# Memory layers on full-array attention products, a head-split output projection and one activation table

## Chip, cores and metric

The kernel runs on one core of a Trainium2 chip. The metric is the device time of one execution in microseconds, as the median of several runs. The core has five engines with their own instruction streams: TensorE (PE; its weight loads are listed as PEld), VectorE (DVE), ScalarE (ACT), GpSimd (POOL) and SyncE (SP). In this kernel TensorE writes to eight PSUM banks of 128x512 float32, and ACT and DVE move the results to SBUF.

## The reference

Four layers with residuals, A, B, A, B, on x of 2048x512 in bfloat16, each after a layer norm without weights. B is linear attention with 32 heads of 16. A is attention with a recurrent memory of 8 rows, 32 heads of 128:

```python
mem = mem0                                  # 8 x 512
for s in range(64):                         # segments of 32 tokens
    h = concat([mem, x[32*s:32*s+32]])      # 40 rows
    q, k, v = h @ Wq, h @ Wk, h @ Wv        # 32 heads of 128
    scores = q @ k.T / sqrt(128)
    scores = where((i < 8) | (i >= j), scores, -1e9)   # i: query row, j: key row
    o = softmax(scores) @ v                 # per head
    o = o @ Wo                              # back to 512
    mem = o[:8]; outs.append(o[8:])
```

The memory rows see all 40 rows; token rows see the memory and the tokens up to themselves. Segment s+1 cannot be projected before segment s's memory rows have come out of Wo.

## The kernel before

**Order of the work.** The kernel lists nodes (`_Prog.add`: engine or engines, function, cost, keys read and written, PSUM tiles). `schedule` is run once for each layer and makes a fixed order for each engine: a list scheduler that takes the ready node with the longest tail by the costs given (`c_act`, `c_dve`, `c_pe`, `c_pe4`), places evictions marked ANY on ACT or DVE, and gives out the eight banks. A node that isn't `urgent` needs three free banks to open a new tile. `emit` then writes the engines' programs, with semaphore waits.

**Tiling of a memory layer** (`a_layer`). A step works on a block of 32 rows: the 8 memory rows and the first 24 tokens of its segment. The last 8 tokens of four segments ("left") make a block of their own, done once for a group of four (`left_block`). With M=32 rows a full array is a quarter used, so nearly everything is put into four column strips of 32 (`tile_position=(0, 32*j)`), which in a group of four run side by side. Heads go as head = 8*j + hh, strip j = 0..3, hh = 0..7, in two halves b.

- `project` (L593): four chunks of the 512 inputs by four strips, 512 wide, so 16 matmuls for each of q, k, v and b.
- `transposed` (L610): the evicted projection is transposed, 16 matmuls of 128 wide, and evicted into qT or kT.
- `mem_attention`: `scores` (L623) of the memory queries against block and left keys, 32 matmuls of 8 wide a half; exponential (L672) on 128x64; sums by matmuls with masks of ones (`sums`, L677 and L680); reciprocal (L684), product (L686); then L689 spreads the probabilities over the four strips with zeros elsewhere (a 4 times wider product with a mask), so that `pvm` (L700, L703) can contract all 128 rows: 32 matmuls a half.
- `x_attention`: the same for the 24+8 token queries: scores 64 matmuls of 24 and 8 wide, exponential (L722), mask (L724), sums (L731, L734), Ln (L738) and Exp of its negative (L740) as reciprocal, products (L742, L744), spreading (L748, twice), and `pvx` 64 matmuls (L759, L763). Its result is for the next step's `out_block`.
- `out_proj` (L781): 32 heads by four strips of 128 output columns: 128 matmuls of 128 wide into a bank of 128x128, evicted to outW in bf16. `next_mem` (L798) selects the 8 memory rows, transposed, into the next block hT. `residual` (L816, L819) does the left output projection and the sum with x once for a group.

Evictions are made by the helper `copy`, so they show as L472 (ACT) or L473 (DVE). Each change between Ln and Exp or Copy brings an ACT_TABLE_LOAD, listed with the line of the activation that needs it.

**Linear layers** (`b_layer`): per tile of 128 tokens a layer norm (transposes L575, in strips), projections with the full array (L885, L892), exponentials and key-value products (L908); then KV and sum products (L927, L933), transposes (L950) and the output projection (L959).

Of the kernel before, what the change touches and what calls it, by code (L numbers as in the profile page):

```python
# [6 lines left out]
F32 = mybir.dt.float32  # L7
ACTF = mybir.ActivationFunctionType
ALU = mybir.AluOpType
# [6 lines left out]
HOP = 0.06  # L16

# [34 lines left out]
class _Node:  # L52
    __slots__ = ("engs", "fn", "cost", "sync", "order", "tiles", "dsem", "dval", "eng", "start", "done",
                 "tail", "sig", "val", "waits", "know", "idx", "nsucc", "succ", "nleft", "urgent")


class _Prog:
    def __init__(self, nc, banks):
        self.nc = nc
        self.nodes = []  # L60
        self.res = {}
        self.banks = banks
        self.dma_tot = {}
        self.sems = {}
        self.done_nodes = []
        self.committed = []
        self.now = {e: 0.0 for e in ENGINES}
        self.bank_owner = [None] * len(banks)
        self.last = {e: None for e in ENGINES}

# [3 lines left out]
    def add(self, engs, fn, cost, reads=(), writes=(), tiles=(), dsem=None, urgent=False):  # L74
        nd = _Node()
        nd.engs = (engs,) if isinstance(engs, str) else tuple(engs)
        nd.cost = cost if isinstance(cost, dict) else {e: cost for e in nd.engs}
        nd.fn = fn
        nd.sync = set()
# [38 lines left out]
    def schedule(self):  # L118
# [72 lines left out]
        def pick_for(e):  # L191
# [7 lines left out]
            while ready[e]:  # L199
# [14 lines left out]
                pick = nd  # L214
                break
# [4 lines left out]
        while n_left:  # L220
# [42 lines left out]
            nd.start = max(tn, rtime(nd))  # L263
            nd.done = nd.start + nd.cost[e]
# [95 lines left out]
def _build_kernel(nc, A_x, A_mem0, A_Wq, A_Wk, A_Wv, A_Wo, A_seg_len, B_wqkv, B_wo, out):  # L360
# [31 lines left out]
    id_sb = sb("id_sb", [128, 128])  # L392
    bo_sb = sb("bo_sb", [128, 128])
    bol_sb = sb("bol_sb", [128, 4, 128])
    bm_sb = sb("bm_sb", [128, 4])
    bm8_sb = sb("bm8_sb", [128, 4, 8, 4])
    mx_sb = sb("mx_sb", [128, 32])
    ml_sb = sb("ml_sb", [128, 32])
    idz_sb = sb("idz_sb", [128, 16, 32])
    selm_sb = sb("selm_sb", [128, 4, 8])  # L400
    maskbd_sb = sb("maskbd_sb", [128, 128])
    onehot8_sb = sb("onehot8_sb", [128, 8], F32)
    A8_sb = sb("A8_sb", [128, 128])
    epsb_sb = sb("epsb_sb", [128, 1], F32)
    mem0_sb = sb("mem0_sb", [128, D])
    memT0_sb = sb("memT0_sb", [128, 4, M])
    st_sb = sb("st_sb", [128, 2, 16], F32)
    xln_sb = sb("xln_sb", [128, 2, D])


    ARENA_N = 29248
# [14 lines left out]
    NI = 5  # L426
    hT = av(3 * 5 * 4 * 32).rearrange("p (r b c x) -> p r b c x", r=3, b=5, c=4)
# [3 lines left out]
    qT = av(2 * 1024).rearrange("p (r h j x) -> p r h j x", r=2, h=8, j=4)  # L431
# [4 lines left out]
    oTl = av(2 * 1024).rearrange("p (r n x) -> p r n x", r=2, n=32)  # L436
    Pm = av(2 * 64).rearrange("p (r a q) -> p r a q", r=2, a=2)
    PRm = av(2 * 64).rearrange("p (r a q) -> p r a q", r=2, a=2)
    Pbm = av(2 * 256).rearrange("p (r a q) -> p r a q", r=2, a=2)
    Px = av(2 * 256).rearrange("p (r h q) -> p r h q", r=2, h=8)  # L440
    PLL = av(2 * 256).rearrange("p (r h q) -> p r h q", r=2, h=8)
    PRx = av(8 * 40).rearrange("p (h q) -> p h q", h=8)
    Pbx = av(8 * 4 * 40).rearrange("p (h j q) -> p h j q", h=8, j=4)
    outW = av(8 * 128).rearrange("p (r x) -> p r x", r=8)
    outWl = av(2 * 128).rearrange("p (r x) -> p r x", r=2)
    Rm = av(2 * 32, F32).rearrange("p (r q) -> p r q", r=2)
    Rx = av(256, F32).rearrange("p (h q) -> p h q", h=8)
    Lx = av(256, F32).rearrange("p (h q) -> p h q", h=8)
# [14 lines left out]
    rd_sb = av(2 * 32, F32).rearrange("p (r x) -> p r x", r=2)  # L463

# [19 lines left out]
    add("sp", lambda s: s.dma_start(mem0_sb[0:M, :], A_mem0[0]), 2.0, writes=["mem0"], dsem="dmem")  # L484
# [5 lines left out]


# [3 lines left out]
    def sel(ap, op, fill, base, pattern, cm, key):  # L495
        pool(lambda g: g.affine_select(out=ap, in_=ap, compare_op=op, fill=fill, base=base, pattern=pattern,
                                       channel_multiplier=cm), writes=[key], reads=[key])
# [4 lines left out]
    pool(lambda g: g.memset(epsb_sb[:, :], EPS_LN), ["epsb"])  # L502

# [3 lines left out]
    pool(lambda g: g.memset(bm_sb[:, :], 1.0), ["bm"])  # L507
    sel(bm_sb[:, :], GE, 0.0, 0, [[-32, 4]], 1, "bm")
    sel(bm_sb[:, :], GE, 0.0, 31, [[32, 4]], -1, "bm")
    pool(lambda g: g.memset(bol_sb[:, :, :], 1.0), ["bol"])  # L510
    sel(bol_sb[:, :, :], GE, 0.0, 0, [[-8, 4], [-32, 4], [0, 32]], 1, "bol")
    sel(bol_sb[:, :, :], GE, 0.0, 7, [[8, 4], [32, 4], [0, 32]], -1, "bol")
    pool(lambda g: g.memset(bm8_sb[:, :, :, :], 1.0), ["bm8"])
    sel(bm8_sb[:, :, 0:4, :], GE, 0.0, 0, [[0, 4], [0, 4], [-32, 4]], 1, "bm8")
    sel(bm8_sb[:, :, 0:4, :], GE, 0.0, 31, [[0, 4], [0, 4], [32, 4]], -1, "bm8")
    sel(bm8_sb[:, :, 4:8, :], GE, 0.0, 0, [[-8, 4], [0, 4], [-32, 4]], 1, "bm8")
    sel(bm8_sb[:, :, 4:8, :], GE, 0.0, 7, [[8, 4], [0, 4], [32, 4]], -1, "bm8")
# [10 lines left out]
    pool(lambda g: g.memset(idz_sb[:, :, :], 0.0), ["idz"])  # L528
    sel(idz_sb[:, :, 24:32], ALU.not_equal, 1.0, 0, [[-8, 16], [-1, 8]], 1, "idz")
    pool(lambda g: g.memset(selm_sb[:, :, :], 0.0), ["selm"])  # L530
    sel(selm_sb[:, :, :], ALU.not_equal, 1.0, 0, [[-32, 4], [-1, 8]], 1, "selm")
    pool(lambda g: g.memset(A8_sb[:, :], 1.0), ["A8"])
    sel(A8_sb[0:8, :], GE, 0.0, 0, [[1, 128]], -16, "A8")
    sel(A8_sb[0:8, :], GE, 0.0, 15, [[-1, 128]], 16, "A8")
# [3 lines left out]
        reads=["A8"], tiles=[tl])  # L538
# [3 lines left out]
        reads=["A8", "id"], tiles=[tl])  # L542
# [7 lines left out]
    add("pe", _m0, 0.2, reads=["mem0", "id"], tiles=[tl])  # L550
# [6 lines left out]
    def layernorm(t):  # L557
        k = ln_no[0] % 2
# [13 lines left out]
        def tr(pe):  # L572
            for c in range(4):
                for q in range(4):
                    r = pe.transpose(tl.bf16()[32 * q:32 * q + 32, 128 * c:128 * c + 128],  # L575
                                     xln_sb[:, k, 128 * c + 32 * q:128 * c + 32 * q + 32], id_sb[:, :],
                                     tile_position=(0, 32 * q))
            return r
        add("pe", tr, c_pe4(16, 128), reads=[("xln", k), "id"], tiles=[tl])
# [3 lines left out]
    def a_layer(layer):  # L583
# [3 lines left out]
        def project(W, key, blk, bkeys, b, urgent):  # L587
            tl = P.tile()
            for c in range(4):
# [6 lines left out]
                add("pe", mm, c_pe4(4, 512), reads=[key] + bkeys, tiles=[tl], urgent=urgent)  # L596
            return tl

        def transposed(W, key, blk, bkeys, b, dst, dkey, urgent):
# [4 lines left out]
            evac(img[:, k, :], lambda: tl.f32()[:, :], 512, tiles=[tl], writes=[("img", k)], urgent=urgent)  # L604
            tt = P.tile()

            def tr(pe):
                for i in range(4):
                    for q in range(4):
                        r = pe.transpose(tt.bf16()[32 * q:32 * q + 32, 128 * i:128 * i + 128],  # L610
                                         img[:, k, 128 * i + 32 * q:128 * i + 32 * q + 32], id_sb[:, :],
                                         tile_position=(0, 32 * q))
                return r
            add("pe", tr, c_pe4(16, 128), reads=[("img", k), "id"], tiles=[tt], urgent=urgent)
            evac(dst.rearrange("p h j x -> p (h j x)"), lambda: tt.bf16()[:, 0:512], 512, tiles=[tt], writes=[dkey],
                 rate=2, urgent=urgent)

        def scores(tl, col, lhs, lhs_keys, rhs, rhs_keys, hhs, w, urgent):

            def mm(pe):  # L620
                for i, hh in enumerate(hhs):
                    for j in range(4):
                        r = pe.matmul(tl.f32()[32 * j:32 * j + 32, col(i):col(i) + w], lhs(hh, j), rhs(hh, j),  # L623
                                      start=True, stop=True, tile_position=(0, 32 * j))
                return r
            add("pe", mm, c_pe4(4 * len(hhs), w), reads=list(lhs_keys) + list(rhs_keys), tiles=[tl], urgent=urgent)

        def left_block(G):
            r3, r2 = G % 3, G % 2
            blk = hT[:, r3, 4, :, :]  # L630
            bk = [("hTl", r3)]
# [9 lines left out]
            for b in range(2):  # L641
                scores(tl, lambda i, b=b: 128 * b + 32 * i, lambda hh, j: kTl[:, r2, hh, j, :], [("kTl", r2, b)],
                       lambda hh, j: qTl[:, r2, hh, j, :], [("qTl", r2, b)], range(4 * b, 4 * b + 4), 32, False)
# [6 lines left out]
        def prepare(G):  # L650
            r3 = G % 3
            tl = layernorm(G)
            src = lambda: tl.bf16()[:, 0:512].rearrange("p (c g x) -> p g c x", c=4, g=4)
            for g in range(4):
                evac(hT[:, r3, g, :, 8:32], lambda g=g: src()[:, g, :, 0:24], 96, tiles=[tl], writes=[("hTx", r3, g)])
            add(ANY, copy(hT[:, r3, 4, :, :].rearrange("p c (g x) -> p c g x", g=4),
                          lambda: tl.bf16()[:, 0:512].rearrange("p (c g x) -> p c g x", c=4, g=4)[:, :, :, 24:32]),
                {"act": c_act(128), "dve": c_dve(128)}, tiles=[tl], writes=[("hTl", r3)])
            left_block(G)

        def mem_attention(s, b):
# [6 lines left out]
            scores(tl, lambda i: 8 * i, lambda hh, j: kT[:, r2, hh, j, :], [("kT", r2, b)],  # L668
                   lambda hh, j: qT[:, r2, hh, j, 0:8], [("qT", r2, b)], hhs, 8, True)
# [346 lines left out]
```

## Time and profile before

| | us |
|---|---|
| median of 3 runs (2885.38 to 2907.2) | 2895.21 |
| profiled execution | 2914.39 |
| its span, first to last instruction | 2912.6 |
| TensorE busy in the span | 2112.6 |
| ACT busy | 1466.8 |
| DVE busy | 1198.0 |

The mean granted clock of TensorE is 0.914. In the profile's groups, "busy" is the summed time of the instructions of a line, "mean ns" one instruction's, and behind the bar stands the idle time of the engine just before them with what ended it. A matmul's own duration holds its fill and drain; what a stream of them costs is read from start to start. In a timeline line, the first number is the start and xN the instructions merged in it.

### The profile page before, as it was taken

Reading aid. Unit: us, or ns where it says so; the run is one execution under the profiler, and the core shown is the slowest. Engines: PE = TensorE matmul, PEld = TensorE weight load, DVE = VectorE, ACT = ScalarE, POOL = GpSimd, SP = SyncE. Lnnn points to the kernel's source line nnn. Section 1 sums busy time; section 2 is a strip of 40 time slices with the busy share of each in tenths; the row PEclk is TensorE's granted clock in tenths of the full one; section 3 lists DMA queues with packets and bytes.
Section 4 is the critical chain, followed back from the end, with each engine's and each line's share of the span. In section 5 each row is a group of like instructions: output and inputs, shape, how many; then the busy total and the mean of one; then the engine's idle time right before and its main releaser. Section 6 shows DMA issues by size and latency. Waiting matters only on the chain.

```text
span 2912.6 us, 180846 instructions
## 1 busy us (share of the span) xinstructions
PE 2112.6 (73%) x87142; PEld 1515.2 (52%) x87166; DVE 1198.0 (41%) x3022; ACT 1466.8 (50%) x3036; POOL 11.1 (0%) x46
## 2 busy tenths in 40 slices
PE   3777777776777776766977777677776777767768
PEld 2555555554555555545545555555554555545555
DVE  2344334343433343433753434343333334334348
ACT  3555445545545454544764554454545444444456
POOL 1000000000000000000000000000000000000000
PEclk9889999999989899998997899989889889998989
DMA  6000000000000000000000000000000000000000
GB/s 261 4 5 4 4 4 4 4 4 4 4 4 4 4 4 5 4 4 16 19 3 4 4 4 4 4 4 4 4 4 4 4 4 4 4 4 4 4 32 30
DMA packets 12938, 36.74 MB, mean 13 GB/s; under 512 B 424, under 2 KB 9648, under 8 KB 10672
## 3 DMA queue, kind: packets, MB, share of 16 engines
q1 hardware_dynamic: 12208, 25.18, 2.4%
q8 instruction: 682, 11.17, 1.6%
q14 instruction: 48, 0.39, 0.0%
HBM read 23.08 MB, written 2.10 MB: 9 GB/s over the span
## 4 chain that ended last, share of the span: by engine, by line
PE 53%; issue 20%; ACT 17%; DVE 8%; DMA 1%; SPq 0%
PE pb L593 21%; PE pb L781 13%; PE pb L623 5%; PE pb L610 4%; ACT L740 4%; ACT arena_sb L472 4%; ACT L738 3%; PE pb L759 2%; DVE arena_sb L748 2%; DVE arena_sb L473 2%; PE pb L703 1%; ACT arena_sb L740 1%; ACT arena_sb L738 1%; PE pb L700 1%; DMA x_sb<-in_A_x_dram 1%
## 5 line engine op out<-in xcount | busy, mean ns | idle before, releaser
L472 ACT ACTIVATE arena_sb<-pb 128x512 bf16<-128x512 f32 (+5 forms) x1829 | 789.2, 455 | 1139.3 <-PE pb L593 309.2
L781 PE MATMUL pb<-Wo_sb,arena_sb 128*32 128x128 bf16 x20736 | 481.5, 248 | 231.6 <-issue 225.8
L593 PE MATMUL pb<-Wq_sb,arena_sb 128*32 128x512 bf16 x5120 | 552.2, 398 | 45.7 <-ACT arena_sb L472 27.8
L473 DVE CAST arena_sb<-pb 128x512 bf16<-128x512 f32 (+3 forms) x584 | 300.6, 516 | 626.6 <-PE pb L593 249.7
L593 PE MATMUL pb<-Wk_sb,arena_sb 128*32 128x512 bf16 x5120 | 548.3, 397 | 12.3 <-issue 12.3
L781 PEld LDWEIGHTS pb<-Wo_sb,arena_sb 128*32 128x32 bf16 x20736 | 396.1, 111 | 274.2 <-issue 261.5
L593 PE MATMUL pb<-Wv_sb,arena_sb 128*32 128x512 bf16 x5120 | 435.4, 395 | 10.8 <-issue 10.7
L623 PE MATMUL pb<-arena_sb 128*32 128x8 bf16 (+1 forms) x17408 | 246.3, 172 | 163.6 <-issue 116.4
L623 PEld LDWEIGHTS pb<-arena_sb 128*32 128x32 bf16 x17408 | 209.8, 94 | 209.6 <-issue 130.3
L610 PE MATMUL pb<-id_sb,arena_sb 128*32 128x128 bf16 x10240 | 252.7, 224 | 71.2 <-ACT arena_sb L472 28.4
L473 DVE COPY arena_sb<-pb 128x512 bf16<-128x512 bf16 (+2 forms) x499 | 185.4, 402 | 232.6 <-PE pb L610 174.6
L593 PEld LDWEIGHTS pb<-Wq_sb,arena_sb 128*32 128x32 bf16 x5120 | 180.7, 100 | 169.8 <-ACT arena_sb L472 43.0
L610 PEld LDWEIGHTS pb<-id_sb,arena_sb 128*32 128x32 bf16 x10240 | 185.9, 98 | 150.8 <-DVE arena_sb L473 51.9
L593 PEld LDWEIGHTS pb<-Wk_sb,arena_sb 128*32 128x32 bf16 x5120 | 178.4, 100 | 116.3 <-issue 34.7
L742 DVE TENSOR_TENSOR arena_sb<-arena_sb 128x256 bf16<-128x256 bf16 x128 | 54.4, 425 | 388.9 <-ACT arena_sb L740 388.8
L748 DVE TENSOR_TENSOR arena_sb<-arena_sb,bm_sb 128x640 bf16<-128x640 bf16 x256 | 203.6, 814 | 4.0
L759 PE MATMUL pb<-arena_sb 128*32 128x128 bf16 x4096 | 157.5, 224 | 26.8 <-issue 25.9
L740 ACT ACT_TABLE_LOAD x126 | 161.7, 1283 | 2.2
L738 ACT ACT_TABLE_LOAD x126 | 161.7, 1283 | 2.2
L763 PE MATMUL pb<-arena_sb 128*32 128x32 bf16 x4096 | 140.1, 183 | 24.0 <-issue 23.9
L703 PE MATMUL pb<-arena_sb 128*32 128x32 bf16 x4096 | 112.5, 180 | 47.7 <-issue 47.7
L593 PEld LDWEIGHTS pb<-Wv_sb,arena_sb 128*32 128x32 bf16 x5120 | 127.6, 97 | 36.1 <-issue 21.1
(102 smaller groups left out, 2301.7 us busy)
## 6 DMA issues: line engine op xcount, KB each, us to landing
Wq_sb<-in_A_Wq_dram SPq DMA_DIRECT2D x1, 4096.0 KB, 12.4
Wk_sb<-in_A_Wk_dram SPq DMA_DIRECT2D x1, 4096.0 KB, 21.9
Wv_sb<-in_A_Wv_dram SPq DMA_DIRECT2D x1, 4096.0 KB, 31.4
Wo_sb<-in_A_Wo_dram SPq DMA_DIRECT2D x1, 4096.0 KB, 35.7
arena_sb<-in_B_wqkv_dram SPq DMA_DIRECT2D x2, 1536.0 KB, 7.2
out_dram<-x_sb SPq DMA_DIRECT2D x16, 128.0 KB, 1.7
x_sb<-in_A_x_dram SPq DMA_DIRECT2D x1, 1920.0 KB, 12.6
arena_sb<-in_B_wo_dram SPq DMA_DIRECT2D x2, 512.0 KB, 8.2
```

The costliest lines, as they stand in the source:

```text
L472: return e.activation(o() if callable(o) else o, i() if callable(i) else i, ACTF.Copy)
L473: return e.tensor_copy(o() if callable(o) else o, i() if callable(i) else i)
L593: r = pe.matmul(tl.f32()[32 * j:32 * j + 32, 0:512], blk[:, c, :], W[:, c, o:o + 512], start=(c == 0), stop=(c == 3), tile_position=(0, 32 ...
L610: r = pe.transpose(tt.bf16()[32 * q:32 * q + 32, 128 * i:128 * i + 128], img[:, k, 128 * i + 32 * q:128 * i + 32 * q + 32], id_sb[:, :], t ...
L623: r = pe.matmul(tl.f32()[32 * j:32 * j + 32, col(i):col(i) + w], lhs(hh, j), rhs(hh, j), start=True, stop=True, tile_position=(0, 32 * j))
L703: r = pe.matmul(pv.f32()[32 * c:32 * c + 32, o:o + 32], vleft[:, g2, 128 * hh + 32 * c:128 * hh + 32 * c + 32], Pbm[:, k, 1, o:o + 32], st ...
L738: add("act", lambda a: a.activation(Lx[:, :, :].rearrange("p h q -> p (h q)"), tl.f32()[:, 256:512], ACTF.Ln), c_act(256), tiles=[tl], wri ...
L740: add("act", lambda a: a.activation(Rx[:, :, :], Lx[:, :, :], ACTF.Exp, scale=-1.0), c_act(256, 0, 1), reads=["Lx"], writes=["Rx"])
L748: add("dve", lambda v, hs=hs: v.tensor_tensor(Pbx[:, hs, :, :], PRx[:, hs, :].unsqueeze(2).to_broadcast([128, 4, 4, 40]), bm_sb[:, :].unsq ...
L759: pe.matmul(o[32 * c:32 * c + 32, :, :], vimg[:, r2, d:d + 32], Pbx[:, hh, :, 0:32], start=True, stop=False, tile_position=(0, 32 * c))
L763: r = pe.matmul(o[32 * c:32 * c + 32, :, 24:32], vleft[:, g2, d:d + 32], Pbx[:, hh, :, 32:40], start=False, stop=True, tile_position=(0, 3 ...
L781: r = pe.matmul(tl.f32()[32 * c:32 * c + 32, 0:128], oT[:, n, :], Wo_sb[:, 8 * j + hh, 128 * c:128 * c + 128], start=(n == 0), stop=(n == 31),
```

## The change

Everything lies in the memory layers, with the set-up and the layer norm helper.

- **Transposes** use the full array: 4 matmuls instead of 16, in the layer norm too.
- **Memory attention**: one product of all four strips' keys with all four strips' queries gives 128x128 scores for four hh; the blocks that pair different heads are set to -1e9 beforehand by a bias product that contracts 16 rows (u16, w16), so that the exponential (128x256 instead of 128x64) gives zeros there and no spreading is needed. Sums are two products with ones, the reciprocal is Ln and Exp of the negative on ACT, and the division is made at the eviction of p*v, which is now 8 full-array matmuls a half.
- **Token attention**: the left queries are copied behind the block's in qT, so scores are 32 matmuls of 32 wide. Sums are 2 full-array products with the block-of-ones mask. Eight products of one 32-row strip each write the divided probabilities straight into the spread image Pbx, whose other places stay zero from the start of the layer. p*v is 16 full-array matmuls.
- **Output projection**: each strip takes its own heads (8*j + hh) and all 512 output columns: 32 matmuls of 512 wide; the four partial sums stay in four strips of 128x512, are evicted as float32r in two halves, and are added up by `next_mem` and `residual`, which are products with selection matrices in float32r. `residual` adds to one bank over the four steps of a group.
- **One table**: `natural_log_exp_and_others` is preloaded on ACT at the start.
- **The planner** gets a mode for each TensorE node (full, col, bias), adds 0.1 us where it changes, and prefers a node of the present mode if its tail is within 0.3 us of the longest.
- **Buffers**: hT 3 to 2, img 5 to 4, oTl 2 to 1, Px 2 to 1, outW 8 of 128 to 3 of 512; A8 and selection scratch lie in kTl, mem0 in vleft. GpSimd makes more masks at the start. No load or store of HBM is added, removed or moved.

The core of the diff:

```diff
+                if pick is None:
+                    pick = nd
+                    if e != "pe" or nd.mode == self.pe_mode:
+                        break
+                    held = item
+                elif nd.tail < pick.tail - MODE_SLACK:
...
+            if e == "pe":
+                if nd.mode != self.pe_mode:
+                    nd.start += PE_SWITCH
+                self.pe_mode = nd.mode
...
+    add("act", lambda a: a.preload_act_table_set("natural_log_exp_and_others"), 1.3)
...
-                    for q in range(4):
-                        r = pe.transpose(tt.bf16()[32 * q:32 * q + 32, 128 * i:128 * i + 128],
-                                         img[:, k, 128 * i + 32 * q:128 * i + 32 * q + 32], id_sb[:, :],
-                                         tile_position=(0, 32 * q))
+                    r = pe.transpose(tt.bf16()[:, 128 * i:128 * i + 128], img[:, k, 128 * i:128 * i + 128], id_sb[:, :])
...
+            def bias(pe):
+                for a in range(2):
+                    r = pe.matmul(tl.f32()[:, 128 * a:128 * a + 128], u16_sb[0:16, :],
+                                  w16_sb[0:16, g, a, :].unsqueeze(1).to_broadcast([16, 4, 32]), start=(a == 0),
+                                  stop=False, skip_group_check=True)
+                return r
+            add("pe", bias, c_pe(2, 128), reads=["u16", "w16"], tiles=[tl], urgent=True, after=early, mode="bias")
+
+            def mm(pe, a, kk):
+                for i, hh in enumerate(hhs):
+                    o = 128 * a + 32 * i
+                    r = pe.matmul(tl.f32()[:, o:o + 32], kk[:, hh, :, :].rearrange("p j x -> p (j x)"),
+                                  qT[:, r2, hh, :, 0:8], start=False, stop=True, skip_group_check=True)
+                return r
...
-            add("dve", lambda v: v.reciprocal(Rm[:, k, :], tl.f32()[:, 64:96]), 0.36, tiles=[tl], writes=[("Rm", k)],
-                urgent=True)
+            add("act", lambda a: a.activation(Rm[:, k, :], tl.f32()[:, 256:384], ACTF.Ln), c_act(128), tiles=[tl],
+                writes=[("Rm", k)], urgent=True)
+            add("act", lambda a: a.activation(Rm[:, k, :], Rm[:, k, :], ACTF.Exp, scale=-1.0), c_act(128, 0, 1),
+                reads=[("Rm", k)], writes=[("Rm", k)], urgent=True)
...
+                    pe.matmul(pv.f32()[:, o], vimg[:, r2, e], Pm[:, k, 0, o], start=True, stop=False)
+                    r = pe.matmul(pv.f32()[:, o], vleft[:, g2, e], Pm[:, k, 1, o], start=False, stop=True)
...
+                            r = pe.matmul(tl.f32()[32 * j:32 * j + 32, 32 * hh:32 * hh + 32], kT[:, r2, hh, j, :],
+                                          qT[:, r2, hh, j, 8:40], start=True, stop=True, tile_position=(0, 32 * j))
...
+            for j in range(4):
+                q = slice(32 * j, 32 * j + 32)
+                add("dve", lambda v, q=q, j=j: v.tensor_tensor(Pbx[q, :, j, 0:32], Px[q, :, :], Rx[q, :, :], ALU.mult),
+                    c_dve(256), reads=["Px", "Rx"], writes=[("Pbx", j)])
...
-                        for c in range(4):
-                            r = pe.matmul(tl.f32()[32 * c:32 * c + 32, 0:128], oT[:, n, :],
-                                          Wo_sb[:, 8 * j + hh, 128 * c:128 * c + 128], start=(n == 0), stop=(n == 31),
-                                          tile_position=(0, 32 * c))
+                    for j in range(4):
+                        r = pe.matmul(tl.f32()[32 * j:32 * j + 32, :], oT[:, 4 * hh + j, :], Wo_sb[:, 8 * j + hh, :],
+                                      start=(hh == 0), stop=(hh == 7), tile_position=(0, 32 * j))
...
+                    for c in (2 * h, 2 * h + 1):
+                        r = pe.matmul(tl.f32()[:, 8 * c:8 * c + 8], outW[:, s % 3, 128 * c:128 * c + 128], selm_sb[:, :],
+                                      start=True, stop=True)
...
+        def residual(G, g):
+
+            if g == 0:
+                res_tile[G] = P.tile()
+            tl = res_tile[G]
+            w = (4 * G + g + 1) % 3
+            add("pe", lambda pe: pe.matmul(tl.f32()[:, :], selx_sb[:, 96 - 32 * g:224 - 32 * g], outW[:, w, :],
+                                           start=(g == 0), stop=False, skip_group_check=True),
+                c_pe(1, 512), reads=[(("outW", w), 0), (("outW", w), 1), "selx"], tiles=[tl])
```

More of the change, by code (lines that the diff above doesn't have):

```diff
@@ L78, in add @@
         nd.fn = fn
-        nd.sync = set()
+        nd.sync = set(after)
         nd.order = set()
@@ L848, in a_layer @@
                 next_mem(s)
[L849 to L850 removed]
+            if s > 0:
+                residual((s - 1) // 4, (s - 1) % 4)
             x_attention(s)
```

380 lines of the change are left out of this document (177 added, 203 removed).

## The prediction

> **What bounds the kernel now.** I read the page first (engine shares, instruction DMA, the chain that ended last), then the busy time by stage, then what TensorE waited for, then the timeline around its longest gaps.
>
> ```profile
> span 2912.6 us, 180846 instructions
> ...
> PE 2112.6 (73%) x87142; PEld 1515.2 (52%) x87166; DVE 1198.0 (41%) x3022; ACT 1466.8 (50%) x3036; POOL 11.1 (0%) x46
> ...
> q8 instruction: 682, 11.17, 1.6%
> ...
> PE 53%; issue 20%; ACT 17%; DVE 8%; DMA 1%; SPq 0%
> ```
>
> TensorE is busy for 73% of the span, and a fifth of the chain that ended last is "issue": TensorE waits there for nothing that the profile shows. The q8 row says that instructions come by DMA, 682 packets of 16 KB. Nearly all belong to TensorE, which runs 174,308 of the 180,846 instructions.
>
> ```profile
> 36.00:1384.00 1348.00, 974.38 (x42648) 705.31 (x42652) 526.27 (x1326) 670.05 (x1404) 0.21 (x2) 0.91 0.03 9
> 1384.00:1471.00 87.00, 77.84 (x936) 48.67 (x940) 71.80 (x183) 60.91 (x116) 0.00 (x0) 0.97 0.04 14
> 1471.00:2824.00 1353.00, 982.46 (x42652) 712.58 (x42652) 527.88 (x1331) 671.66 (x1403) 0.21 (x2) 0.90 0.02 5
> 2824.00:2912.00 88.00, 77.64 (x916) 48.55 (x928) 70.46 (x181) 59.84 (x112) 0.00 (x0) 0.97 0.10 34
> ```
>
> The columns are the stretch, its length, then PE, PEld, DVE, ACT and POOL busy, and the granted clock. A start of 36 us, two memory layers of 1350 us, two linear layers of 88 us. Each memory layer is 64 recurrent steps, so one step takes 21.1 us, with TensorE busy for 15.2 and idle for 5.8.
>
> ```profile
> PE pb L781 <- issue: 225.8, 152, 2.4
> PE pb L623 <- issue: 116.4, 81, 2.6
> PE pb L700 <- issue: 48.0, 33, 2.4
> PE pb L703 <- issue: 47.7, 29, 2.4
> ...
> PE pb L593 <- issue: 40.0, 38, 2.4
> ```
>
> These five rows (total us, times, longest) make 477.9 us, 3.7 us in each of the 128 steps. The gaps sit where matmuls are short (scores, output projection). The timeline shows what they are:
>
> ```profile
> 634.63 0.82 PE L623 MATMUL pb<-arena_sb 128*32 128x8 bf16 x78 [2.02 <-issue]
> 635.34 1.47 PE L781 MATMUL pb<-Wo_sb,arena_sb 128*32 128x128 bf16 x48
> 636.58 0.26 PE L700 MATMUL pb<-arena_sb 128*32 128x32 bf16 x2
> 638.49 0.21 PE L700 MATMUL pb<-arena_sb 128*32 128x32 bf16 x2 [1.65 <-issue]
> ```
>
> Between the end of one gap and the end of the next lie 78+48+2 = 128 matmuls and as many weight loads: 256 instructions, about one packet of the q8 row (11.17 MB / 180,846 is 62 bytes each). The next packet was ready 3.86 us after the block began (634.63 to 638.49); TensorE had used the block up in 1.95 us plus the last tail. So a block of 128 matmuls costs at least about 3.9 us however short they are, 30 ns a matmul. **TensorE's instruction stream, not its arithmetic, sets the pace of the dense stretches.** The Trainium skill, "Runtime: NRT & Kernel Launch", section "Instruction fetch mechanics", says that refills come in blocks of 256 instructions and that crossing a block is mostly hidden; the rows agree on the block and disagree on the hiding. By its rule the idle would have another cause and stay; that is a rival below.
>
> **TensorE's prices.** Start to start, in the two tiling modes:
>
> ```profile
> 626.13 0.41 PE L593 MATMUL pb<-Wq_sb,arena_sb 128*32 128x512 bf16 x4
> 626.35 0.41 PE L593 MATMUL pb<-Wk_sb,arena_sb 128*32 128x512 bf16 x4
> ...
> 627.22 0.41 PE L610 MATMUL pb<-id_sb,arena_sb 128*32 128x128 bf16 x16 [0.24 <-DVE arena_sb L473]
> 627.45 0.39 PE L593 MATMUL pb<-Wv_sb,arena_sb 128*32 128x512 bf16 x4
> ```
>
> ```profile
> 1432.67 1.06 PE L885 MATMUL pb<-arena_sb 128*128 128x128 bf16 x16
> 1433.56 1.03 PE L892 MATMUL pb<-arena_sb 128*128 128x512 bf16 x4
> ...
> 1435.32 1.03 PE L892 MATMUL pb<-arena_sb 128*128 128x512 bf16 x4
> 1436.28 0.63 PE L575 MATMUL pb<-id_sb,xln_sb 128*32 128x128 bf16 x32
> 1436.84 0.35 PE L908 MATMUL pb<-arena_sb 128*128 128x129 bf16 x3
> ...
> 1443.92 0.35 PE L933 MATMUL pb<-arena_sb 128*128 128x8 bf16 x8
> 1444.14 0.38 PE L927 MATMUL pb<-arena_sb 128*128 128x128 bf16 x4
> ```
>
> With 32 columns of weights, four 512-wide matmuls take 0.216 us together (54 ns each) and a 128-wide one 0.23/16 = 14.4 ns; the 78 narrow ones above took 0.71/78 = 9 ns each. With the full array, 128-wide costs 0.89/16 = 55.6 ns, 8-wide 0.22/8 = 27 ns, and 512-wide by width four times the first, 0.216. Nothing is gained per column by the full array; a matmul simply does four times as much.
>
> **A step now, by these prices.** Per step (one quarter of the left block in each): 120 projections x 54 ns = 6.5; 286 of 128 wide (transposes, output projection, p*v of the tokens, residual) x 14.4 = 4.1; 256 narrow x 9 = 2.3; four 256-wide sums 0.1: 13.0 us of streaming. Idle 5.8. The clock:
>
> ```profile
> 614.70:635.20 20.50, 14.65 (x750) 10.47 (x742) 8.39 (x22) 10.46 (x21) 0.00 (x0) 1.00 0.02 4
> 635.20:642.00 6.80, 4.77 (x208) 4.30 (x202) 0.57 (x2) 3.64 (x6) 0.00 (x0) 0.50 0.02 5
> ...
> 639.79 1.79 PE L781 MATMUL pb<-Wo_sb,arena_sb 128*32 128x128 bf16 x58
> ```
>
> After the two fetch gaps above the clock was granted at 0.50, and the 58 matmuls took (1.79-0.27)/58 = 26 ns instead of 14.4. A mean of 0.905 in these layers means 19% of the time at half clock, 4.0 us of a step, of which 72% busy: 1.45 us lost. 13.0+5.8+1.45 = 20.3 of 21.1; 0.8 is left for the ends of bursts.
>
> **A step after the change.** 284 matmuls for 666. Projections unchanged, 6.47. Transposes 21 full x 55.6 = 1.17. Output projection 40.5 of 512 wide x 54 = 2.18 (for 162 x 14.4 = 2.33: the columns are the same, the instructions a quarter). Bias 4, sums 4, token p*v 8 and next_mem 4, all taken at 55.6: 1.11. Narrow full-array ones (memory scores 16, p*v 16, left columns 9) x 27 = 1.1. Token scores 40 x 9 = 0.36. Token sums 0.11. Residual 1.25 x 0.216 = 0.27. Streaming: **12.8 us, no less than the 13.0 of now.** The gain is not there.
>
> Fetch: 284 matmuls are 2.2 blocks a step; at 16 us a block lasts 7 us, and a block cannot hold 128 short ones, since only 124 of a step are not 512 wide and they are spread over it. 3.9 us suffices; I take 0.1 for the 3.7 (bounds 0 and 0.8).
>
> Mode switches: new. Full to 32 columns: 1436.28-1435.32 = 0.96 for four of 0.216, so 0.10 extra; back: 0.56 for 32 of 14.4 ns, 0.10 extra. The plan changes between projections, transposes, scores, token scores, output projection and next_mem, and the bias product contracts 16 rows; I count 16 changes, 1.6 us (10 to 24: 1.0 to 2.4). The Trainium skill speaks against the change here: "TensorEngine Tiling (Array Packing)", section "Key Properties", says that a change of tiling mode drains TensorE, without a figure; the trace agrees, at 0.10. If only the 128 cycles that "TensorE: Matmul & The Clock Gate" gives for a drain were paid ("Step-by-step: what each phase is for"), an estimate of 53 ns at its 2.4 GHz, the total would be 95 us lower.
>
> Float32r products (next_mem, residual) have no row. Below, the bf16 price I used; above, twice that for twice the bytes: +0.5 us a step. I take the lower, the same widths being the nearest row, and keep +0.5 for the range.
>
> Other engines:
>
> ```profile
> L738 ACT ACT_TABLE_LOAD x126 | 161.7, 1283 | 2.2
> L740 ACT ACT_TABLE_LOAD x126 | 161.7, 1283 | 2.2
> ...
> L472 ACT ACTIVATE arena_sb<-pb 128x512 bf16<-128x512 f32 x706 | 413.8, 596 | 343.5 <-PE pb L593 309.2 <-PE pb L680 14.3 <-PE pb L892 2.9
> L748 DVE TENSOR_TENSOR arena_sb<-arena_sb,bm_sb 128x640 bf16<-128x640 bf16 x256 | 203.6, 814 | 4.0
> ...
> L722 ACT ACTIVATE arena_sb<-pb 128x256 bf16<-128x256 f32 x128 | 49.1, 383 | 59.6 <-PE pb L623 58.5
> L742 DVE TENSOR_TENSOR arena_sb<-arena_sb 128x256 bf16<-128x256 bf16 x128 | 54.4, 425 | 388.9 <-ACT arena_sb L740 388.8
> ```
>
> The table loads take 1.283 us each; with Ln and Exp in one table at least these 252 (323 us, 2.5 a step) go. The spreading products go (L748: 203.6). In come, per step, four 256-wide products at 0.425 and four of 64 at about half, the copies into qT, two wider exponentials (0.383), Ln and Exp for the memory rows and an output eviction four times as wide: about 5 us a step by these rows, a little more than the removed arithmetic. ACT and DVE together stay near half busy, beside TensorE's work. Uncovered, they would lengthen the recurrence, which is the second case.
>
> The recurrence after: q and k projections 64 x 54 = 3.45; eviction with handover 0.8; transposes 0.4; eviction 0.6; scores and exponential 0.7; sums, Ln, Exp, product 1.25; the second half of the output projection 0.86; eviction 0.6; next_mem and eviction 0.7: 9.4 us. Under 16, so TensorE is still the bound, but the cover is thinner; of today's 2.1 us of other idle I keep 1.3 (0.5 to 3.0). The residual tile now holds one of 8 banks for four steps, several rings are shorter, and the left output projection must precede the next group's eviction into the single oTl, behind which stand, on ACT or DVE, the next step's evictions that the transposes wait for: all in that upper bound.
>
> Clock: without gaps of 2 us, 0.3 instead of 1.45 (0 to 1.2). Ends of bursts 0.1, the rest being in the switch price.
>
> Sum: 12.8+0.1+1.6+1.3+0.3+0.1 = **16.2 us a step**. 128 of them 2074; start 36, since the longer GpSimd set-up (some 70 short instructions for 46, about 17 us) lies behind the loading of x and the weights (uncovered: +6); linear layers 84 each (their 16 tiles lose two switches a tile): 2278. The profiled execution took 2914.39 us, 1.8 more than its span, and the median of the three runs is 2895.21, a factor of 0.9934: (2278+1.8) x 0.9934 = **2265 us**.
>
> **The rivals.** Each time is 36+168 us plus 128 steps, in the same scale.
> - *The recurrence becomes the bound.* A dozen handovers, each behind one operation of 0.4 us on ACT or DVE, and waits in TensorE's fixed order: 18.0 a step, 2493 us. For it: ACT and DVE hold 25% of the present chain. Against: 9.4 leaves room, and table loads and L748 no longer stand in the queues. Chance 0.16.
> - *The waits vanish too.* Eleven switches, no cold clock, 0.6 idle: 14.6, 2061 us. Against: TensorE's order is fixed ahead. 0.10.
> - *The tables still load.* If the preloaded table is not kept, 2.5 us a step stays on ACT and half of it on the recurrence: 17.4, 2417 us. 0.05.
> - *The issue idle is not fetch.* Then 3.7 stays: 19.8, 2722 us; with waits of 2.7, near their bound, 21.2 and 2900 us, no change. For it: the rows name no releaser; against: the spacing of 256. 0.04. It is what the rule of the Trainium skill on instruction fetch, above, would give.
> - *The clock stays low: slower.* If the many short waits leave TensorE's activity too thin, more streaming runs at half clock, as in the stretch at 635 us. It decides from 5.3 us lost a step, 41% of the streaming; at 50% the step is 22.3, 3040 us. Against: from 614.70 to 635.20 the clock stayed full with TensorE busy for only 14.65 of 20.5 us. 0.05.
>
> **How the numbers follow.** Forecast 0.60, its own range 15.2 to 17.3 a step (2137 to 2404). The range for 8 in 10 goes to 2050 (half of the third case) and to 2540 (past the recurrence). About 1% can be told from no change: faster 0.93, within it 0.02 (half of the fetch rival), slower 0.05.
>
> **What would show it.** About 38,000 matmuls and 300 instruction packets; issue idle below 50 us in all; memory layers near 1037 us; clock 0.96 or more; one or two table loads; 0.1 us at each change of tiling. Wrong, if issue idle stays in the hundreds with fewer packets, if the clock falls below 0.85, or if TensorE idles over 4 us a step on ACT or DVE.

## The result and the profile after

The changed kernel takes **2160.9 us** (median of 4, 2159.93 to 2161.59) where the kernel before took 2895.66: a ratio of 0.7461, 95% interval 0.7433 to 0.7490. The forecast was 2265 with a range of 2050 to 2540. Its direction and its cause held; it was 104 us too high.

The page of the changed kernel: its span, engine shares, instruction queue and the chain that ended last.

```profile
span 2158.2 us, 83024 instructions
...
PE 2079.3 (96%) x37982; PEld 1163.5 (54%) x37982; DVE 1201.2 (56%) x3287; ACT 1159.7 (54%) x3112; POOL 14.8 (1%) x74
...
q8 instruction: 297, 4.87, 0.9%
...
PE 94%; DVE 2%; DMA 2%; ACT 1%; issue 0%; SPq 0%
```

Matmuls fell from 87142 to 37982 and instruction packets from 682 to 297, and TensorE's busy time did not: 2112.6 us then, 2079.3 now. What went is idle time, 800 us down to 79, and "issue" is no longer in the chain. The stages (length, busy PE, PEld, DVE, ACT, POOL, granted clock):

```profile
0.00:48.00 48.00, 0.35 (x3) 0.19 (x4) 3.87 (x9) 2.06 (x4) 14.35 (x70) 1.00 0.99 376
48.00:1016.00 968.00, 961.29 (x18224) 531.99 (x18224) 524.99 (x1453) 532.72 (x1453) 0.21 (x2) 1.00 0.02 4
1016.00:1102.00 86.00, 78.81 (x768) 50.49 (x768) 73.02 (x188) 46.03 (x101) 0.00 (x0) 0.95 0.06 20
1102.00:2072.00 970.00, 960.97 (x18228) 531.45 (x18228) 528.08 (x1459) 533.26 (x1456) 0.21 (x2) 1.00 0.01 3
2072.00:2158.00 86.00, 77.90 (x763) 49.34 (x761) 71.28 (x182) 45.58 (x100) 0.00 (x0) 0.96 0.12 42
```

A memory layer takes 968 us, 15.1 a step, and TensorE is busy in all but 7 us of it, at full clock. The three longest of TensorE's waits (total us, times, longest) all lie outside the steps:

```profile
PE pb L614 <- DVE arena_sb L607: 36.7, 4, 24.9
PE pb L577 <- POOL arena_sb L524: 22.8, 1, 22.8
PE pb L921 <- DMA arena_sb<-in_B_wqkv_dram: 5.2, 2, 2.7
```

Now TensorE's own work is the bound. The timeline around the first `next_mem` shows two of its prices:

```profile
69.59 0.39 PE L630 MATMUL pb<-Wk_sb,arena_sb 128*32 128x512 bf16 x4
69.91 0.39 PE L827 MATMUL pb<-selm_sb,outW_sb 128*128 128x8 f32 x2
70.23 0.40 PE L630 MATMUL pb<-Wq_sb,arena_sb 128*32 128x512 bf16 x4
```

Four projection matmuls cost 0.216 us and take 0.32 to the next start: 0.10 for the change of mode, as forecast. The two float32r matmuls, 8 wide, take 0.32 with their change of mode.

### The profile page after: what moved, and what is told of

It is laid out like the page before. It is cut to its first block, busy times and chain, and to the rows that moved or that the text cites. A ratio compares the mean times of both kernels' runs of the same rounds, so it can differ in the third digit from the quotient of the medians.

```text
span 2158.2 us, 83024 instructions
## 1 busy us (share of the span) xinstructions
PE 2079.3 (96%) x37982; PEld 1163.5 (54%) x37982; DVE 1201.2 (56%) x3287; ACT 1159.7 (54%) x3112; POOL 14.8 (1%) x74
## 4 chain that ended last, share of the span: by engine, by line
PE 94%; DVE 2%; DMA 2%; ACT 1%; issue 0%; SPq 0%
PE pb L630 42%; PE pb L808 14%; PE pb L646 8%; PE pb L792 4%; PE pb L827 3%; PE pb L921 3%; PE pb L710 3%; PE pb L701 3%; PE pb L842 2%; PE pb L722 2%; DMA x_sb<-in_A_x_dram 2%; PE pb L735 2%; PE pb L759 2%; PE pb L914 1%; PE pb L736 1%; PE pb L771 1%
## 5 line engine op out<-in xcount | busy, mean ns | idle before, releaser
L498 ACT ACTIVATE arena_sb<-pb 128x512 bf16<-128x512 f32 (+6 forms) x1410 | 673.2, 492 | 458.7 <-PE pb L630 269.7
L499 DVE CAST arena_sb<-pb 128x512 bf16<-128x512 f32 (+2 forms) x541 | 312.3, 578 | 237.6 <-PE pb L793 142.5
L808 PE MATMUL pb<-Wo_sb,arena_sb 128*32 128x512 bf16 x5184 | 350.1, 381 | 0.0
L780 DVE TENSOR_TENSOR arena_sb<-arena_sb 32x256 bf16<-32x256 bf16 x512 | 213.3, 417 | 133.6 <-ACT arena_sb L776 121.7
L499 DVE COPY arena_sb<-pb 128x512 bf16<-128x512 bf16 (+1 forms) x543 | 205.8, 399 | 137.8 <-PE pb L646 134.3
L646 PE MATMUL pb<-id_sb,arena_sb 128*128 128x128 bf16 x2560 | 216.7, 220 | 0.0
L646 PEld LDWEIGHTS pb<-id_sb,arena_sb 128*128 128x128 bf16 x2560 | 145.0, 97 | 103.2 <-issue 41.6
L808 PEld LDWEIGHTS pb<-Wo_sb,arena_sb 128*32 128x32 bf16 x5184 | 119.7, 95 | 102.4 <-issue 20.7
L792 PE MATMUL pb<-arena_sb 128*128 128x128 bf16 x1024 | 115.2, 218 | 4.0 <-DVE arena_sb L782 4.0
L710 PE MATMUL pb<-arena_sb 128*128 128x32 bf16 x2048 | 118.6, 177 | 0.0
L793 PE MATMUL pb<-arena_sb 128*128 128x32 bf16 x1024 | 105.6, 178 | 0.0
```

The source lines that it names most:

```text
L498: return e.activation(o() if callable(o) else o, i() if callable(i) else i, ACTF.Copy)
L499: return e.tensor_copy(o() if callable(o) else o, i() if callable(i) else i)
L646: r = pe.transpose(tt.bf16()[:, 128 * i:128 * i + 128], img[:, k, 128 * i:128 * i + 128], id_sb[:, :])
L710: r = pe.matmul(tl.f32()[:, o:o + 32], kk[:, hh, :, :].rearrange("p j x -> p (j x)"), qT[:, r2, hh, :, 0:8], start=False, stop=True, skip_ ...
L780: add("dve", lambda v, q=q, j=j: v.tensor_tensor(Pbx[q, :, j, 0:32], Px[q, :, :], Rx[q, :, :], ALU.mult), c_dve(256), reads=["Px", "Rx"], ...
L792: pe.matmul(o, vimg[:, r2, e], Pbx[:, hh, :, 0:32], start=True, stop=False)
```

## The experiments

The theory (fetch): blocks of 256 instructions that come no faster than about one in 3.9 us made TensorE wait; fewer instructions for the same columns are the gain. The rival (tables): the loads of activation tables on ACT lengthened the recurrence, and one table is the gain. A third (streaming): the full array streams less. The first four runs set them against each other, by one part alone in the kernel before and by one part undone in the changed one.

The trace of the kernel before ties the gaps to the fetch: it has the landing time of each instruction packet (q8). All 375 of TensorE's issue gaps over 0.5 us end 1.19 to 1.61 us after a packet landed, while the packets themselves come 4.2 us apart in the mean; 238 of the gaps end 127 or 128 matmuls after the one before. Those 238 blocks took 3.3 to 5.9 us, median 3.75, so the one pair from which the prediction took 3.9 us is typical.

**One table alone, in the kernel before.**

```diff
+    add("act", lambda a: a.preload_act_table_set("natural_log_exp_and_others"), 1.3)
```

> The kernel before with the activation table preloaded and nothing else changed. Fetch theory (TensorE waits for blocks of 256 instructions, the tables load beside that): about 0 to 100 us faster, 2800 to 2895, issue idle of TensorE still above 450 us. Table theory (the loads on ACT lengthen the recurrence and were the loss): the 435 us of loads go from ACT and 160 to 320 us from the time, 2575 to 2735.

2759.4 us, ratio 0.950 (0.946 to 0.953): 144 us faster, between the two. The largest of TensorE's waits:

```profile
PE pb L783 <- issue: 235.4, 154, 2.4
PE pb L625 <- issue: 129.7, 96, 2.6
PE pb L702 <- issue: 53.5, 34, 2.6
PE pb L705 <- issue: 50.0, 29, 2.6
```

All four are issue. Summed over the whole view, TensorE's issue idle rose from 575 to 637 us and its waits for others fell from 216 to 73. So the loads did stand behind those waits, and when they are gone the blocks take part of the gain back. TensorE's busy time falls too, from 2112.6 to 2044.6 us, as the mean clock rises from 0.914 to 0.925.

**The wide output projection alone, in the kernel before.**

```diff
-                        for c in range(4):
-                            r = pe.matmul(tl.f32()[32 * c:32 * c + 32, 0:128], oT[:, n, :],
-                                          Wo_sb[:, 8 * j + hh, 128 * c:128 * c + 128], start=(n == 0), stop=(n == 31),
-                                          tile_position=(0, 32 * c))
+                        r = pe.matmul(tl.f32()[32 * j:32 * j + 32, :], oT[:, n, :], Wo_sb[:, 8 * j + hh, :],
+                                      start=(hh == 0), stop=(hh == 7), tile_position=(0, 32 * j))
```

> The kernel before with the output projection in 512-wide matmuls, 32 for 128, and nothing else changed. It evicts only the first 128 columns of each strip and leaves out the sum over the strips. The columns that stream are the same, 15552 matmuls and as many weight loads fewer (about 120 packets). Fetch theory: most of the 226 us of issue idle at this line goes, with some half clock: 225 to 330 us faster, 2565 to 2670. Table or recurrence theory, and a theory of streaming: within 1% of 2895.

2603.4 us, ratio 0.897 (0.893 to 0.900): 300 us faster, inside the fetch theory's range and far from the others'. 122 packets fewer, the same columns. Its page and TensorE's first waits:

```profile
q8 instruction: 560, 9.18, 1.5%
...
PE 52%; ACT 24%; issue 13%; DVE 10%; DMA 1%; SPq 0%
```

```profile
PE pb L623 <- issue: 77.7, 51, 2.6
PE pb L703 <- issue: 46.9, 35, 2.0
PE pb L623 <- ACT arena_sb L672: 46.6, 21, 2.4
PE pb L610 <- DVE arena_sb L473: 43.0, 71, 1.3
PE pb L780 <- issue: 42.6, 32, 2.4
```

The 226 us at the output projection (L780 in this kernel) are down to 43. Issue idle in all is 319, and waits for other engines rose to 274: with fewer blocks to wait for, TensorE seems to meet ACT and its tables more often. The mean clock rose from 0.914 to 0.959. The Trainium skill, "Runtime: NRT & Kernel Launch", section "Instruction fetch mechanics", calls the crossing of a block mostly hidden; here it isn't, at 2.5 us a packet saved (300/122), with what the higher clock gains included.

**Both parts, in the kernel before.**

> The kernel before with both single parts, the preloaded table and the 512-wide output projection (again only the first 128 columns of each strip are evicted and the sum over the strips is left out). Fetch theory: two separate losses, so their gains of 144 and 300 us add: 2420 to 2490, TensorE waiting for no other engine and 250 to 350 us of issue idle left, in the scores and products that are still cut small. Rival (one loss seen twice, the recurrence): little more than the larger, 2560 to 2610.

2365.2 us, ratio 0.819 (0.816 to 0.823): 528 us faster, more than the sum of 444 and below the 2420 of the fetch theory's range, which neither side had. Issue idle 366 us, other waits 64:

```profile
PE 1941.1 (82%) x71614; PEld 1291.8 (54%) x71614; DVE 1204.1 (51%) x3022; ACT 1037.5 (44%) x2698; POOL 11.1 (0%) x46
...
PE 80%; issue 16%; DVE 2%; DMA 2%; ACT 0%; SPq 0%
```

This fits two losses that cover each other: alone, each part hands about 60 us of its gain to the other's waits (575 to 637, 216 to 274). Together they don't. The changed kernel is 204 us faster still: the 366 us of issue idle go, by this account because its attention products and transposes are a half to a quarter as many, and TensorE is busy for 138 us more. The changes of mode come in there (1.7 us a step, some 220 us, as shown below) and half clock goes out (0.962 to 0.994). No run takes these parts one by one.

**The table undone, in the changed kernel.**

```diff
-    add("act", lambda a: a.preload_act_table_set("natural_log_exp_and_others"), 1.3)
```

> The changed kernel without the preload. Three Ln and three returns to Exp a step can bring six loads of 1.28 us, 7.7 us on ACT beside the 8.2 it has, just over the 15 us of TensorE. Fetch theory: TensorE keeps its few instructions, so the loss is what ACT adds, 1 to 5 us a step, 2290 to 2800, with TensorE waiting for ACT and no issue idle. Table theory (the table is the gain): all of it is lost, 2890 or more.

3075.1 us, ratio 1.059 (1.055 to 1.062): **slower than before the change.** This is far above the fetch theory's 2800. The size is what the table theory asked for, while the mechanism is the one that the fetch theory named: no issue idle at all, 666 us of waits for other engines, and a clock of 0.887. Groups of lines (count, busy us, mean ns) and TensorE's waits:

```profile
L724 ACT ACT_TABLE_LOAD x254 | 325.9, 1283 | 4.5
L726 ACT ACT_TABLE_LOAD x154 | 197.6, 1283 | 2.7
...
L773 ACT ACT_TABLE_LOAD x104 | 133.4, 1283 | 1.8
```

```profile
PE pb L721 <- ACT arena_sb L716: 179.2, 133, 2.7
PE pb L807 <- DVE arena_sb L738: 171.7, 121, 2.3
```

The new reciprocal of the memory rows is Ln and Exp (L724, L726 here), so its loads come into the recurrence itself. ACT is busy for 2190 us of a span of 3067, and these two waits come about once a step (133 and 121 times). The same preload is worth 144 us in the kernel before and 914 here: few instructions and one table are both needed for the gain. The Trainium skill, "ScalarE: Activation LUTs", section "Table sets: the hidden batching unit", says that one set holds both functions and that Ln followed by Exp needs one load; the trace agrees only where that set is preloaded (one load in the changed kernel, 813 of 1.283 us without).

**The output projection cut small again, in the changed kernel**, with the order of work untouched.

```diff
-                    for j in range(4):
-                        r = pe.matmul(tl.f32()[32 * j:32 * j + 32, :], oT[:, 4 * hh + j, :], Wo_sb[:, 8 * j + hh, :],
...
+                    for c in range(4):
+                        cs = slice(128 * c, 128 * c + 128)
+                        for j in range(4):
+                            r = pe.matmul(tl.f32()[32 * j:32 * j + 32, cs], oT[:, 4 * hh + j, :],
+                                          Wo_sb[:, 8 * j + hh, cs], start=(hh == 0 and c == 0), stop=(hh == 7),
...
```

> The changed kernel with each 512-wide matmul of the output projection cut into four of 128, in the same order of work and with the same columns and heads: 122 matmuls more a step. Fetch theory: 128 of them stream in 1.8 us and a block takes 3.9, so 1.3 to 2.7 us a step come back as issue idle and half clock: 2330 to 2510, issue idle 150 to 300 us, clock under 0.97. Streaming theory (columns count, not instructions): within 1% of 2161.

2314.8 us, ratio 0.798 (0.794 to 0.802), 154 us slower than the changed kernel for 122 packets more. Issue idle comes back where nothing else was changed, but 96 us of it and not 150:

```profile
PE pb L810 <- issue: 59.3, 55, 1.9
...
PE pb L759 <- issue: 19.8, 18, 1.6
```

The clock falls to 0.981 and busy time rises by 56 us. The columns are equal and instructions are the only thing added, so the columns are ruled out as the cause. The expected range was missed on all three counts, by 15 us, 54 us and 0.011 of clock. The likely reason is that the planner lays projections between the two halves: in this trace, stretches of 128 matmuls that hold 50 to 79 of the output projection hold 22 projections as well (median) and last 4.4 us, more than a block takes to come.

**What the changed kernel's time now consists of.** If TensorE never waits, whatever leaves it must leave the time. Three edits take away a small thing each; one adds some. Each group of kernels was timed at another time than the changed kernel, and the kernel before, timed beside each, had medians from 2893 to 2910 us, so a few us of time show nothing without the trace.

```diff
-                    r = pe.matmul(tl.f32()[:, 128 * a:128 * a + 128], u16_sb[0:16, :],
-                                  w16_sb[0:16, g, a, :].unsqueeze(1).to_broadcast([16, 4, 32]), start=(a == 0),
+                    r = pe.matmul(tl.f32()[:, 128 * a:128 * a + 128], u16_sb[:, :],
+                                  w16_sb[:, g, a, :].unsqueeze(1).to_broadcast([128, 4, 32]), start=(a == 0),
...
-            add("pe", bias, c_pe(2, 128), reads=["u16", "w16"], tiles=[tl], urgent=True, after=early, mode="bias")
+            add("pe", bias, c_pe(2, 128), reads=["u16", "w16"], tiles=[tl], urgent=True, after=early)
```

> The changed kernel with the bias product contracted over all 128 rows (the added rows multiply zeros), so that it stays in the full-array mode. TensorE-bound account: it never waits, so what leaves TensorE leaves the time; one change of mode fewer for each of two bias products a step, 0.09 us each: 20 to 30 us faster, 2131 to 2141. Rival (the drain at a change of mode hides in other waits): no change, 2155 to 2165.

2138.2 us, 23 faster: changes of mode (counted in the trace, by the shapes of the matmuls that follow each other) fall from 2276 to 2012, and 264 x 0.095 is 25.

```diff
-    outW = sb("outW_sb", [128, 3, 512], F32R)
+    outW = sb("outW_sb", [128, 3, 512])
```

(and the same for outWl, selm, selx and sell)

> The changed kernel with the evicted partial sums and the selection matrices in bf16 instead of float32r; the partial sums are rounded to bf16. TensorE-bound account: next_mem 4 x (124-27) ns and residual 1.25 x (322-216) ns leave each step, 0.52 us: 55 to 75 us faster, 2086 to 2106. Rival (float32r costs what bf16 does, as the prediction took it): no change.

2109.9 us, 51 faster, a little under the range. The same place in its timeline:

```profile
68.30 0.39 PE L630 MATMUL pb<-Wk_sb,arena_sb 128*32 128x512 bf16 x4
68.62 0.21 PE L827 MATMUL pb<-selm_sb,outW_sb 128*128 128x8 bf16 x2
68.75 0.40 PE L630 MATMUL pb<-Wq_sb,arena_sb 128*32 128x512 bf16 x4
```

0.13 us for the pair, where float32r took 0.32: 0.095 a matmul, four in a step, 49 us in 128 steps. The `residual` saves as well: from its start to the next there are 0.32 us in float32r and 0.22 in bf16 (medians where a transpose follows), 14 us in 128 matmuls. TensorE's busy time falls by 65 us, inside the expected range (about 5 us of that are matmuls missing from this trace); its waits for other engines rise by 6 us, and a few us stay open.

```diff
-PE_SWITCH = 0.1
-MODE_SLACK = 0.3
+PE_SWITCH = 0.0
+MODE_SLACK = 0.0
```

> The changed kernel with a planner that does not see tiling modes (no charge for a change, no preference). Account: each change of mode costs 0.1 us of a TensorE that never waits; changes rise from 17.8 a step to some 24 to 32, so 0.6 to 1.4 us a step: 2240 to 2340. Rival (the drain is small beside the order of the work): within 1% of 2161.

2226.1 us, 65 slower. Changes rose from 2276 to 2904 (22.7 a step, under the 24 expected); 628 x 0.1 is 63. The price held, the count was guessed too high, and TensorE waits no more than before (79 us for 74, start and linear layers included).

The third small thing is the start, where the first tile of x lands late. It comes first in the program's list, but the planner sorts the loads by their tails, and in the changed kernel it put this tile behind all four weights. In the kernel before, only Wq, Wk and Wv went ahead of it. So a load was moved after all, by the planner. SyncE's timeline, kernel before and changed kernel:

```profile
2.38 7.49 SPq L483 DMA_DIRECT2D x_sb<-in_A_x_dram  x1
9.91 2.10 SPq L487 DMA_DIRECT2D Wo_sb<-in_A_Wo_dram  x1
```

```profile
2.38 7.45 SPq L513 DMA_DIRECT2D Wo_sb<-in_A_Wo_dram  x1
9.87 29.62 SPq L509 DMA_DIRECT2D x_sb<-in_A_x_dram  x1
```

Issued at 2.38 and landed 31.2 us later, the tile was there at 33.6 us before; issued at 9.87 and landed 36.1 us later, it is there at 46.0 now. The first attempt to bring it forward held back only Wq, Wk and Wv:

```diff
-        add("sp", lambda s, W=W, v=v: s.dma_start(W[:, :, :], v), 12.0, writes=[nm], dsem="d" + nm)
+        add("sp", lambda s, W=W, v=v: s.dma_start(W[:, :, :], v), 12.0, reads=[("x", 0)], writes=[nm], dsem="d" + nm)
```

> The changed kernel with the three projection weights' loads held back until the first tile of x has landed (they then start some 2 us later). The first tile now lands at 46 us behind 16 MB of weights, and the first projection starts at 49. Account: the first projection starts at 15 to 20, the second waits for Wk at about 25, Wv at 35 and Wo at 46; step 0 ends about 10 to 25 us earlier: 2136 to 2151. Rival (the load of all weights sets the start anyway): within 3 us of 2161.

2156.1 us, 5 faster, which is little more than nothing: a miss. The tile landed in 2.2 us, but Wo, not held back, went ahead of Wq, which landed 22.9 us after its issue, so that the first projection starts at 26.0 us. With the same `reads` on the loads of Wo and the rest of x:

> The changed kernel with all four weights' loads and the rest of x held back until the first tile of x has landed, so that the order of issue stays Wq, Wk, Wv, Wo. Account: Wq lands at about 15 us, Wk at 25, Wv at 35, Wo at 45; the first next_mem comes at 52 to 58 us for 69.9, and the time falls by as much: 2143 to 2150. Rival (the loads' total sets the start): the first next_mem at 62 or later, 2153 or more.

2147.7 us, 13 faster, as expected, and the first `next_mem` comes at 53.0 us for 69.9. The first tile's load (last column: us from issue to landing) in the changed kernel and in this one:

```profile
x_sb<-in_A_x_dram SPq DMA_DIRECT2D x1, 128.0 KB, 36.1
```

```profile
x_sb<-in_A_x_dram SPq DMA_DIRECT2D x1, 128.0 KB, 2.2
```

**Together.** The bias, bf16 and x edits in one kernel:

> The changed kernel with the three parts together: bias product over 128 rows, partial sums in bf16, first tile of x alone. TensorE-bound account: what leaves TensorE adds up, 23+51+10 to 17 us: 2070 to 2078. Rival (another engine takes over soon after 2.1 ms): less than two thirds of the sum, 2103 or more, with TensorE waiting for ACT or DVE.

2072.6 us, ratio 0.7174 (0.7153 to 0.7194): 88 us faster than the changed kernel, where 23+51+13 is 87. Then the planner's preference at 0.6 us of tail:

```diff
-MODE_SLACK = 0.3
+MODE_SLACK = 0.6
```

> The same with the planner's preference widened from 0.3 to 0.6 us of tail. Account: fewer changes of mode, 0.1 us each, with no wait in their place: 0 to 40 us faster than the kernel without it, by 0.1 us for each change that is gone. Rival (work of the recurrence comes later and TensorE then waits for it): slower by the same order.

**2042.1 us, ratio 0.7066 (0.7042 to 0.7091)**, the fastest of all, 119 us under the changed kernel. Changes of mode fall from 2016 to 1440, worth 58 us at 0.1, and 30 are gained: TensorE's waits rise by 18 us, in small ones at the ends of the recurrence:

```profile
PE pb L630 <- DVE arena_sb L499: 11.7, 54, 0.3
PE pb L827 <- ACT outW_sb L498: 11.7, 31, 0.5
```

Some 10 us stay unexplained. The chain that ended last runs over DVE for 21% of the span now, for 10% with a preference of 0.3 us and 2% in the changed kernel: the recurrence comes close to being the bound.

## Why the prediction was right, and where it was off

- *TensorE's instruction stream sets the pace; streaming doesn't fall.* Right, and shown from both sides: 122 packets taken from the kernel before are worth 300 us, 122 put into the changed one cost 154, at equal columns. Busy time fell by 33 us of 2112, issue idle from 575 to 0. Of the 15.1 us of a step, 1.75 are changes of mode and 0.5 is the extra price of float32r, which leaves the 12.8 us of streaming that were forecast.
- *Fetch 0.1 us a step.* None is left.
- *Mode switches, 16 at 0.10 us.* 17.8 at 0.095 to 0.10, 1.7 us a step for 1.6. Right.
- *Float32r at the price of bf16.* Too low: 0.095 us more for each `next_mem` matmul and 0.11 for each `residual`, 0.5 a step. That is the upper bound of +0.5.
- *"Of today's 2.1 us of other idle I keep 1.3."* **This is the term that was furthest off.** In the changed kernel it is 0.1 us a step (7 us in 968). Some 0.75 of the 2.1 was issue idle too: the five rows of the prediction hold 478 of its 575 us, and fetch was priced by them alone. The rest was waits for other engines. The sum took the table loads away on ACT and left the waits that came from them on TensorE; one table alone in the kernel before shows that two thirds of those waits were the loads (216 to 73 us), and most of the rest is start and linear layers. With the clock term (0.3 forecast, full clock measured) this makes up 1.5 us of the step; float32r gives 0.5 back, and the other terms are within 0.1: 16.2 forecast, 15.1 measured; 2074 us forecast for the 128 steps, 1938 measured. The start gave back 12 us and the linear layers 4.
- *The start, 36 us.* 48. The GpSimd set-up was hidden, as said (it ends at 22.7); the first tile of x landed 12 us later than before, because the planner issued it 7.5 us later, behind Wo. The prediction took the order of the loads as unchanged.
- *Linear layers 84 each.* 86.
- *The tables still load* was priced at 2417 us, a step of 17.4. The condition did not occur, but made to occur it costs 3075: the price put half of 2.5 us on the recurrence and left out that the change adds two Ln and two Exp a step there, and so more loads than before (813 for 339). Its chance was small, but its cost was misjudged by 658 us.
- *The waits vanish too* (0.10) was the nearest rival, no further from the result than the forecast (100 us and 104), and its waits came true; its eleven switches came only with the planner's wider preference, in a kernel of 2042 us.

## What to carry to other kernels

Count TensorE's instructions by blocks: where 128 matmuls with their weight loads take less than about 4 us, try first to cut the same columns into wider matmuls; here that alone was worth 300 us at equal columns. When two losses run side by side, one part alone shows less than its worth, and one part missing can cost more than the whole gain; so try pairs. Once an engine never waits, price every small thing on it (0.1 us a change of tiling mode, 0.1 for a float32r matmul), since most of each leaves the time: 23 us of 25 and 51 of 63 here, but only 30 of 58 once other engines were waited for again. And look at the order in which a planner really issues the loads, not at the order of the program.

## What was not expected of the hardware

- Fetch idle, at gaps of up to 2.6 us, went with half clock: the share lost to the clock (1 less the mean granted clock) was 0.086 in the kernel before (575 us of issue), 0.041 with the wide output projection alone (319), 0.038 with both parts (366) and 0.006 in the changed kernel (none). It isn't issue idle alone: with one table alone it was 0.075 at 637 us, and without the preload, waits for other engines of up to 2.7 us went with 0.113. The Trainium skill, "TensorE: Matmul & The Clock Gate", section "What's actually happening", has the clock fall after an idle window of about 3.4 us; here no single gap in the steps was that long.
- A float32r matmul of 8 columns took about 0.095 us more than one in bf16; its weight load is listed at 188 ns in the changed kernel, a bf16 one of the same 128 columns (L710) at 96.
- A load of 128 KB, issued behind 16 MB, landed after 36.1 us; issued ahead of everything it landed after 2.2 us, also where a load of 4 MB was issued 0.4 us behind it (the first attempt above).
